# Five moves of order in a fused attention and feed-forward kernel: spread stores, another order of splits, another choice of banks

## The chip, the cores and the metric

One core of a Trainium2 chip runs the kernel. The metric is the device time of one execution in microseconds (us); less is better. TensorE (PE in the profile) does the matmuls, VectorE (DVE), ScalarE (ACT) and GpSimd (POOL) the elementwise work, and SyncE (SP) issues every DMA of this kernel, in the order of the program.

## The reference, cut to what matters

The input x has 2048 rows of 576 features. The output is a mix of two branches: `g*a + (1-g)*b`, with g a sigmoid of a dot product of each row with a gate vector.

- Branch a is attention with a compressive memory: 32 heads of 18 features and 4 segments of 512 rows. Each segment has causal softmax attention within itself, and reads a memory M (and its normaliser z) summed over the segments before it. The two are mixed per head and multiplied by `wo`.
- Branch b is a gated feed-forward layer: `(silu(x @ w_gate) * (x @ w_up)) @ w_down`, with 4608 hidden features.

All inputs and the output are float32. The kernel keeps that precision on TensorE by splitting each operand into a rounded high part and a remainder, a "split": ACT copies the high part, DVE subtracts it from the source to get the low part. Three products (high by high, high by low, low by high) then stand for one.

## The kernel before, in words

**First stage (lines 283 to 685).** The projections for queries, keys and values, and the memory. Near its end the operands for the first half of the feed-forward layer are made: `w_make` splits the weights, `first_sum` (POOL) and `first_split` (ACT and DVE, through `split`, lines 131 to 133) make the seven x operands.

**Main stage (lines 688 to 1126).** The feed-forward layer runs over `seq`: two halves of the rows (1024 each), and in each half 36 units f of 128 hidden features, so 72 units. One unit is seven products (`seven`, line 1010, a Strassen-like scheme: seven products of sums and differences instead of eight). One `seven` is six matmuls at line 1015 and one at line 1018, all with 512 columns. After each `seven` (and twice after the sixth) the unit calls `tick`, so eight ticks, k = 0 to 7. A tick issues some DMAs and then calls `beat`.

**The beat (line 959)** is where the order of the work is written by hand. It first runs the functions that are due (`defer(k, fn)` puts fn into the list of the k-th beat from now; items of one list run in the order in which they were deferred). Then, if groups of the down projection are waiting, it runs some of them (`SHARE[k]`: none in beats 0 and 1, two in beats 2 and 3, three in beats 4 to 7); between them it advances the attention generator `att_gen` by one step. A unit with groups takes 12 attention steps; a unit without groups about 2 to 3, since only five of its beats count and each earns 0.57 (first half) or 0.47 (second half) of a step.

**Groups.** Every third unit f (`q == 0`) `feed` puts 16 groups on the list: the down projection of the three units before. A group (`down_parts`, line 848) is nine matmuls of line 862 into one bank, then DVE adds the bank to `ya` (line 872) and the bank is free.

**Attention.** 64 units u of 5 logits tiles each. `att_gen` takes six steps for a unit, n = 0 to 5. A step does `p_bank` (line 753: DVE cast, POOL subtraction), `e_bank` (ACT exponentials, line 742), `s_bank` (line 717: the matmuls of the logits, line 724, and the DVE reduction of line 730; in steps 0 to 4), `v_unit` (line 763: the 40 small matmuls of lines 772 and 773 with the values, then a DVE reduction, line 779; in step 5, for the unit before) and `x_bank` (line 759: a DMA transpose into a `pt` tile, of which there are seven).

**Banks.** The PSUM has eight banks. Banks 0 to 2 serve the seven products. `group_tile` takes the least recently taken of banks 3, 4 and 7. `ts_tile`, for logits and values, takes the least recently taken of 5, 6, 7, 3, 4 when no groups wait; of 5, 6, 7 while all 16 groups still wait (beats 0 and 1); of 5 and 6 afterwards. A tile of `ts_tile` counts as taken four ticks of the clock later than it was, a group's one.

**Between the halves.** After unit 35 of the first half come ten beats of their own (lines 1109 to 1117, `BREAK`), in which the last 16 groups of the half run. The first of these beats also runs three groups at once in two cuts: the products of the first two units, then those of unit 35, whose split is due in that same beat. Meanwhile `x_second` (line 979) makes the x operands of the second half. Its four tables give the beat of each step, with offset 0 on the first tick of unit 35, 8 on the first of the ten beats and 18 on the first tick of the second half: `LOADS` (raw pieces of x from memory; z = 0 and 1 are two sets), `SUMS` (POOL, line 991), `PARTS` (the splits: ACT line 132, DVE line 133). The ten beats' groups also leave eight finished tiles of `ya` on the list `stores` (line 874); `tick` issues them all when k is 0. The weights of units 0 and 1 of the second half come ready-made from memory (`w_fetch`, line 704, into `wo_` tiles, source `wc`); the last of unit 0, for its seventh product, is issued in the first tick of the second half, behind the stores.

**Last stage.** The output projection, 16 tiles of rows (lines 1128 to 1161).

Of the kernel before, what the change touches and what calls it, by code (L numbers as in the profile page):

```python
# [26 lines left out]
NSEG = 4  # L27
# [8 lines left out]
CH = 3  # L36
# [12 lines left out]
SHARE = (0, 0, 2, 2, 3, 3, 3, 3)  # L49
BREAK = 10  # L50
LOADS = ((-3, 0, 0), (-2, 0, 1), (3, 1, 0), (4, 1, 3), (4, 0, 3), (5, 0, 2), (5, 1, 1), (6, 1, 2))
SUMS = ((2, 0, 1), (9, 0, 4), (10, 1, 1), (11, 1, 4), (13, 1, 2), (14, 1, 6), (17, 0, 2), (18, 0, 6))
PARTS = ((1, 0, 0), (4, 0, 1), (10, 1, 0), (12, 1, 5), (12, 1, 3), (13, 1, 1), (14, 1, 2), (15, 1, 4), (16, 1, 6),
         (16, 0, 5), (17, 0, 3), (18, 0, 2), (19, 0, 4), (20, 0, 6))
FIRST = (9, 10, 11, 15, 16, 17, 18)
SLOT = (0, 3, 2, 1, 4, 6, 5)
RPOS = (0, 1, 4, 2, 5, 6, 3)
# [9 lines left out]
def gated_mix(ctx, tc, xT, xrest, wf, wfr, wfh, wd, wv, wo, beta, cmask, ident, bmask, out):  # L67
# [44 lines left out]
    y_tile = banks(2)  # L112
    taken = {}
    clock = [0]

    def soonest(ids, held):
        n = min(ids, key=lambda i: taken.get(i, 0))
# [2 lines left out]
        return n  # L120

    def ts_tile(shape=(P, L)):
        ids = (5, 6, 7, 3, 4) if not groups else (5, 6, 7) if groups[0][0] < FT // CH - 1 and len(groups) == 16 else (5, 6)
        return ps.tile(list(shape), F32, name=f"bank{soonest(ids, HELD)}")

    def group_tile(shape=(P, L)):
# [157 lines left out]
    with ExitStack() as st:  # L284
# [249 lines left out]
        def first_split(j, z):  # L534
            XO[j][z] = x_slot(SLOT[j], z)
            split(XO[j][z][:, 0], XO[j][z][:, 1], rx[{1: (0, z), 4: (1, z), 2: (1, 2 + z), 6: (0, 2 + z)}[j]])
# [144 lines left out]
        flush()  # L681
        while start[0][0] < 8:
            start.pop(0)[1]()
        for z in range(2):
            first_split(6, z)


    with ExitStack() as st:
# [3 lines left out]
        def defer(k, fn):  # L692
            while len(due) < k:
                due.append([])
            due[k - 1].append(fn)
# [100 lines left out]
        def att_gen():  # L796
            N = 12 * NB

            def at(t):
                return 5 * (t // 6) + t % 6 if 0 <= t < N and t % 6 < 5 else None  # L800

            for tau in range(N + 10):
                u, n = divmod(tau, 6)
                if n == 2 and sends:
                    nc.sync.dma_start(*sends.pop(0))
                if 1 <= n <= 3 and u + 1 < 2 * NB:
                    for d in stack_loads(u + 1)[3 * n - 3:3 * n]:
                        nc.sync.dma_start(*d)
                if n == 2 and u > 1 and u % 2 == 1 and (u - 3) // 2 < NB:
                    o_step((u - 3) // 2)  # L810
                z = at(tau - PL)
                if z is not None:
                    p_bank(z)
                z = at(tau - 1)
                if z is not None:
                    e_bank(z)
                z = at(tau)
                if z is not None:
                    s_bank(z)
                if n == 5 and 1 <= u <= 2 * NB:  # L820
                    v_unit(u - 1)
                    if u % 4 == 1 and u // 4 + 1 < 4 * NSEG:
                        v_fetch(u // 4 + 1)
                z = at(tau - XL)
                if z is not None:
                    x_bank(z)
                yield
            for z in sends:
                nc.sync.dma_start(*z)
# [191 lines left out]
        draw = {}  # L1021
        for o, fn in start:
            defer(o - 7, fn)
        for pos, (half, f) in enumerate(seq):
            if f == 0:
                yas[half] = yp.tile([P, 8, D], F32, name="ya")
# [1 line left out]
            nxt = seq[pos + 1] if pos + 1 < len(seq) else None  # L1028
            if q == 0 and f:
                groups += feed(half, f - 1)  # L1030
            plan = []
            if not nxt:
                plan.append((3, lambda: early.append(c_tr(*tiles.pop(0)))))
# [17 lines left out]
            def tick():  # L1051
                k = step[0]
                step[0] += 1
                if k == 0:
                    while stores:
                        nc.sync.dma_start(*stores.pop(0))
                if half == 0:
                    if (q, k) in ((0, 3), (1, 3), (2, 2)):
                        draw[f] = d_load(f)
# [156 lines left out]
```

## Time and profile before

| what | value |
|---|---|
| time, median of 3 runs | 1736.47 us (1733.69 to 1738.83) |
| the profiled execution's own time | 1734.02 us |
| its span, first to last instruction | 1732.2 us |
| granted TensorE clock, mean | 0.999 |
| busy: PE, DVE, ACT, POOL | 1713.1, 1373.7, 1092.4, 936.7 us |
| mean share of the DMA engines on the core's queue | 76.6% |

A row of the timeline gives the start (us from the span's start), the duration, engine, line, operation, what is written and read, how many instructions were merged, and in brackets the idle time before it with what ended it. TensorE's matmuls are pipelined: a matmul of 512 columns is shown with about 0.39 us, though the next one starts about 0.23 us after it. So a wait of TensorE is read from start to start; the bracket shows only what is left after the shown end. In the list of waits each row gives the engine and line that waited, what it waited for, the total in us, how often, and the longest.

In the first half unit 0 starts at 220.87 us; the ten beats between the halves run from about 925.4 to 947.7 us, and the second half's unit 0 starts at 947.69 us.

### The profile page before, as it was taken

Reading aid. Unit: us, or ns where it says so; the run is one execution under the profiler, and the core shown is the slowest. Engines: PE = TensorE matmul, PEld = TensorE weight load, DVE = VectorE, ACT = ScalarE, POOL = GpSimd, SP = SyncE. Lnnn points to the kernel's source line nnn. Section 1 sums busy time; section 2 is a strip of 40 time slices with the busy share of each in tenths; the row PEclk is TensorE's granted clock in tenths of the full one; section 3 lists DMA queues with packets and bytes.
Section 4 is the critical chain, followed back from the end, with each engine's and each line's share of the span. In section 5 each row is a group of like instructions: output and inputs, shape, how many; then the busy total and the mean of one; then the engine's idle time right before and its main releaser. Section 6 shows DMA issues by size and latency. Waiting matters only on the chain.

```text
span 1732.2 us, 34907 instructions
## 1 busy us (share of the span) xinstructions
PE 1713.1 (99%) x11868; PEld 1479.3 (85%) x11868; DVE 1373.7 (79%) x3231; ACT 1092.4 (63%) x2195; POOL 936.7 (54%) x1194
## 2 busy tenths in 40 slices
PE   9999999999999999999999999999999999999999
PEld 7899978888888888887888788888888888888899
DVE  6667588888898889898989677788788777888655
ACT  7766585776677577667756756665765576566511
POOL 4424645666666556565666455555555555555221
PEclk9999999999999999999999999999999999999999
DMA  8654499999898898897979976876778677766544
GB/s 285 227 194 154 146 311 191 223 218 193 208 227 194 178 213 198 190 194 200 206 150 260 273 161 146 183 180 157 157 181 181 137 161 182 163 144 166 160 146 137
DMA packets 524002, 328.05 MB, mean 189 GB/s; under 512 B 411184, under 2 KB 460336, under 8 KB 523824
## 3 DMA queue, kind: packets, MB, share of 16 engines
q1 hardware_dynamic: 523824, 325.83, 76.6%
q8 instruction: 93, 1.52, 0.4%
q14 instruction: 85, 0.70, 0.1%
HBM read 165.76 MB, written 76.09 MB: 140 GB/s over the span
## 4 chain that ended last, share of the span: by engine, by line
PE 80%; ACT 6%; DVE 6%; DMA 3%; issue 2%; POOL 1%; SPq 1%; DVEq 0%; ACTq 0%; POOLq 0%
PE bank L1015 31%; PE bank L862 25%; PE bank L155 10%; PE bank L1018 5%; PE bank L724 4%; PE bank L772 2%; PE bank L773 1%; ACT L1092 1%; PE bank L410 1%; DVE scr L730 1%; DVE hl L957 1%; DVE p L756 1%; PE bank L456 1%; ACT L1008 1%; DVE xo L133 1%
## 5 line engine op out<-in xcount | busy, mean ns | idle before, releaser
L757 POOL TENSOR_TENSOR p<-pe,p 128x512 f16<-128x512 f32 x320 | 374.0, 1169 | 451.0 <-DVE p L756 431.3
L862 PE MATMUL bank<-dw,hh 128*128 128x320 f32 (+1 forms) x2304 | 489.7, 305 | 2.6 <-DVE ya L872 2.1
L862 PEld LDWEIGHTS bank<-dw,hh 128*128 128x128 f32 x2304 | 380.5, 190 | 16.7 <-DVE ya L872 5.7
L742 ACT ACTIVATE pe<-bank,mb 128x512 f32<-128x512 f32 (+3 forms) x512 | 246.0, 522 | 218.7 <-DVE mb L730 213.3
L862 PE MATMUL bank<-dw,hl 128*128 128x320 f32 (+1 forms) x1152 | 340.3, 295 | 0.2 <-DVE hl L133 0.2
L730 DVE CUSTOM_DVE_ANT_0 scr<-bank,cm 128x512 bf16<-128x512 f32 (+3 forms) x512 | 246.5, 481 | 7.8 <-PE bank L724 1.1
L862 PEld LDWEIGHTS bank<-dw,hl 128*128 128x128 f32 x1152 | 217.9, 189 | 0.4 <-DVE hl L133 0.4
L872 DVE TENSOR_TENSOR ya<-bank,ya 128x320 f32<-128x320 f32 x352 | 157.6, 453 | 71.5 <-PE bank L862 70.6
L1018 PE MATMUL bank<-xr,rh 128*128 128x512 f32 x504 | 196.5, 390 | 0.0
L750 POOL TENSOR_SCALAR_AFFINE_SELECT pe<-pe 128x256 f32<-128x256 f32 (+1 forms) x320 | 151.1, 473 | 30.4 <-ACT pe L742 20.1
L756 DVE CAST p<-pe 128x512 f16<-128x512 f32 x320 | 149.2, 466 | 0.0
L260 POOL TENSOR_TENSOR ws<-raw 128x256 f32<-128x256 f32 x140 | 123.5, 882 | 17.3 <-DMA raw<-in_wf_dram 5.1
L724 PE MATMUL bank<-kst,qst 108*128 108x512 bf16 (+3 forms) x512 | 125.5, 306 | 0.0
L1018 PEld LDWEIGHTS bank<-xr,rh 128*128 128x128 f32 x504 | 94.7, 188 | 20.5
L957 DVE TENSOR_TENSOR hl<-row,hh 128x512 fp32r<-128x512 f32 x120 | 101.9, 849 | 10.8 <-ACT hh L956 10.5
L1085 ACT ACTIVATE row<-bank 128x512 f32<-128x512 f32 x72 | 43.1, 598 | 83.9 <-PE bank L1018 83.8
L1092 ACT ACT_TABLE_LOAD x72 | 92.4, 1283 | 1.3
L1090 DVE TENSOR_TENSOR row<-bank,row 128x512 f32<-128x512 f32 x72 | 49.6, 689 | 54.6 <-ACT bank L1089 54.4
L1008 ACT ACT_TABLE_LOAD x70 | 89.8, 1283 | 1.0
L1089 ACT ACTIVATE bank<-bank 128x512 f32<-128x512 f32 x72 | 42.0, 584 | 67.2 <-PE bank L1018 66.8
L155 PE MATMUL bank<-xo,qhi 128*128 128x512 f32 x264 | 83.1, 396 | 0.3 <-ACT vps L395 0.3
L1075 ACT ACTIVATE bank<-bank 128x512 f32<-128x512 f32 x72 | 41.6, 578 | 66.2 <-PE bank L1018 66.2
(2167 smaller groups left out, 4137.6 us busy)
## 6 DMA issues: line engine op xcount, KB each, us to landing
raw<-in_wf_dram SPq DMA_DIRECT2D x140, 256.0 KB
rh<-rc SPq DMA_DIRECT2D x72, 336.0 KB
dc<-dw SPq DMA_DIRECT2D x36, 576.0 KB
dw<-dc SPq DMA_DIRECT2D x36, 576.0 KB
stk<-q SPq DMA_DIRECT2D x32, 384.0 KB
draw<-in_wd_dram SPq DMA_DIRECT2D x36, 288.0 KB
rc<-rt SPq DMA_DIRECT2D x42, 224.0 KB
vd<-vps SPq DMA_DIRECT2D x8, 912.0 KB
```

The costliest lines, as they stand in the source:

```text
L155: nc.tensor.matmul(t, st[n], mv[n], start=(n == 0), stop=(n == 13))
L260: (nc.gpsimd.tensor_sub if sub else nc.gpsimd.tensor_add)(src[j], p(), q())
L724: nc.tensor.matmul(t[:, c:c + w], qs[:KR, pr, P * i:P * i + P], ks[:KR, pr, 0:w], start=True, stop=True)
L730: nc.vector.tensor_tensor_reduce(scr[:, :w], t[:, c:c + w], cm[:, L - w:L], -SCALE, 3.0e38, OP.add, OP.min, m[:, k:k + 1])
L742: nc.scalar.activation(pe[:, c:c + w], t[:, c:c + w], AF.Exp, bias=m[:, k:k + 1], scale=SCALE)
L750: nc.gpsimd.affine_select(d, d, pattern=pat, compare_op=OP.is_ge, fill=0.0, base=0, channel_multiplier=1)
L756: nc.vector.tensor_copy(p[:, 0], pe)
L757: nc.gpsimd.tensor_sub(p[:, 1], pe, p[:, 0])
L862: nc.tensor.matmul(ts[m], p, q[:, cs], start=(n == 0), stop=(n == 3 * CH - 1))
L872: nc.vector.tensor_add(ya[:, i, cs], t, ya[:, i, cs])
L1015: nc.tensor.matmul(t, w[:, p, z], x[z][:, q], start=first and n == 0, stop=False, skip_group_check=True)
L1018: nc.tensor.matmul(t, rem[:, RPOS[j]], XR[j], start=False, stop=True, skip_group_check=True)
```

## The change: what it does

1. **Stores.** `tick` issues one waiting store in each odd tick, instead of all of them in tick 0. The eight stores go out in ticks 1, 3, 5 and 7 of units 0 and 1 of the second half.
2. **The order of x.** `SUMS` and `PARTS` get other offsets and another order. Ten splits lie in the ten beats instead of nine, and two follow in ticks 0 and 1 of the second half instead of three in ticks 0 to 2. The first two splits of the set z = 0 move to offsets 8 and 9. All sums lie before offset 17, two of them earlier than before. `LOADS` stays.
3. **Bank 7 first.** The first tile that `ts_tile` gives out after `feed` is bank 7 (unless bank 7 is the one taken last, or the groups are the half's last); after that, while groups wait, only banks 5 and 6.
4. **Values ahead of the next step's logits.** Where no groups wait at step 5, `v_unit` (with the `v_fetch` that hangs on it) is held and runs in step 0 of the next unit, after that step's exponentials and ahead of its logits. Where groups wait, it stays in step 5.
5. **The last split of x.** `first_split(6, z)`, two splits, ran at the end of the first stage; it is now due in the second beat of unit 0, so after that unit's second product.

```diff
-SUMS = ((2, 0, 1), (9, 0, 4), (10, 1, 1), (11, 1, 4), (13, 1, 2), (14, 1, 6), (17, 0, 2), (18, 0, 6))
-PARTS = ((1, 0, 0), (4, 0, 1), (10, 1, 0), (12, 1, 5), (12, 1, 3), (13, 1, 1), (14, 1, 2), (15, 1, 4), (16, 1, 6),
-         (16, 0, 5), (17, 0, 3), (18, 0, 2), (19, 0, 4), (20, 0, 6))
+SUMS = ((2, 0, 1), (9, 0, 4), (11, 0, 2), (12, 1, 1), (13, 1, 4), (14, 0, 6), (14, 1, 2), (16, 1, 6))
+PARTS = ((1, 0, 0), (4, 0, 1), (8, 0, 5), (9, 0, 3), (10, 1, 0), (11, 1, 5), (12, 1, 3), (13, 0, 4), (14, 0, 2),
+         (15, 1, 1), (16, 1, 4), (17, 1, 2), (18, 0, 6), (19, 1, 6))
...
+    fed = []
...
     def ts_tile(shape=(P, L)):
-        ids = (5, 6, 7, 3, 4) if not groups else (5, 6, 7) if groups[0][0] < FT // CH - 1 and len(groups) == 16 else (5, 6)
+        ids = (5, 6) if groups else (5, 6, 7, 3, 4)
+        if fed and groups[0][0] < FT // CH - 1 and max(taken, key=taken.get) != 7:
+            ids = (7,)
+        fed.clear()
         return ps.tile(list(shape), F32, name=f"bank{soonest(ids, HELD)}")
...
-        for z in range(2):
-            first_split(6, z)
...
+            held = []
             for tau in range(N + 10):
...
+                if n == 5 and 1 <= u <= 2 * NB:
+                    held.append(u)
+                if held and (groups or n == 0):
+                    v = held.pop()
+                    v_unit(v - 1)
+                    if v % 4 == 1 and v // 4 + 1 < 4 * NSEG:
+                        v_fetch(v // 4 + 1)
                 z = at(tau)
                 if z is not None:
                     s_bank(z)
-                if n == 5 and 1 <= u <= 2 * NB:
-                    v_unit(u - 1)
-                    if u % 4 == 1 and u // 4 + 1 < 4 * NSEG:
-                        v_fetch(u // 4 + 1)
...
+        for z in range(2):
+            defer(2, lambda z=z: first_split(6, z))
...
                 groups += feed(half, f - 1)
+                fed.append(f)
...
-                if k == 0:
-                    while stores:
-                        nc.sync.dma_start(*stores.pop(0))
+                if k % 2 and stores:
+                    nc.sync.dma_start(*stores.pop(0))
```

## The prediction

> **What bounds the kernel now.** I read the page's busy times and chain first, then the list of TensorE's waits, then the timeline around each long one.
>
> ```profile
> PE 1713.1 (99%) x11868; PEld 1479.3 (85%) x11868; DVE 1373.7 (79%) x3231; ACT 1092.4 (63%) x2195; POOL 936.7 (54%) x1194
> ...
> PE 80%; ACT 6%; DVE 6%; DMA 3%; issue 2%; POOL 1%; SPq 1%; DVEq 0%; ACTq 0%; POOLq 0%
> ```
>
> ```profile
> PE bank L1015 <- DMA wo__13415<-wc: 3.0, 1, 3.0
> PE bank L862 <- DVE ya L872: 2.1, 3, 0.9
> PE bank L1015 <- ACT bank L1075: 1.7, 5, 0.6
> PE bank L1015 <- DVE bank L1082: 1.6, 2, 1.1
> ...
> PE bank L1015 <- DVE xo L133: 0.9, 1, 0.9
> PE bank L772 <- DMA pt<-p: 0.9, 1, 0.9
> ```
>
> TensorE is busy 99% of the span and holds 80% of the chain that ended last. The change takes no matmul away, so all it can win is TensorE's waits, and these rows hold most of them: about ten microseconds in single, short pieces. The sum below is made from start to start in the timeline, since the list shows less than a wait costs.
>
> **The last split of x (part 5).** In unit 0 the third product adds to the bank that line 1075 copies, and waits for that copy.
>
> ```profile
> 223.93 0.39 PE L1018 MATMUL bank<-xr,rh 128*128 128x512 f32 x1
> 224.87 1.66 PE L1015 MATMUL bank<-xo,wo__2473 128*128 128x512 f32 x6 [0.56 <-ACT bank L1075]
> ```
>
> ```profile
> 223.20 1.14 ACT L132 ACTIVATE xo<-ph 128x512 fp32r<-128x512 f32 x2
> 224.25 0.57 ACT L1075 ACTIVATE bank<-bank 128x512 f32<-128x512 f32 x1
> ```
>
> ```profile
> 224.24 1.41 DVE L133 TENSOR_TENSOR xo<-ph,xo 128x512 fp32r<-128x512 f32 x2
> ...
> 226.87 0.70 DVE L1082 TENSOR_TENSOR bank<-bank,row 128x512 f32<-128x512 f32 x1 [0.88 <-PE bank L1018]
> ```
>
> The two high copies (1.14 us) stand right ahead of it on ACT. Moved two beats on, they leave line 1075 free to run from 223.20 to 223.8, before the second product ends at 224.15. The gap from 223.93 to 224.87 is 0.94 us where two matmuls without a wait start 0.22 apart (394.72 and 394.94 below): **0.7 us** gained. Behind them, DVE's two subtractions (1.41 us) now stand between the second product and line 1082. That instruction was idle for 0.88 us before, and its user is the fifth product, one product later; the cover is thin, so the bounds are 0 and 0.8.
>
> **Bank 7 first (part 3).** Of the groups in beat 3, the first is the half's third.
>
> ```profile
> 267.66 0.39 PE L1018 MATMUL bank<-xr,rh 128*128 128x512 f32 x1
> 268.13 0.56 PE L862 MATMUL bank<-dw,hh 128*128 128x320 f32 x2
> ```
>
> ```profile
> 389.57 0.39 PE L1018 MATMUL bank<-xr,rh 128*128 128x512 f32 x1
> 390.60 0.56 PE L862 MATMUL bank<-dw,hh 128*128 128x320 f32 x2 [0.65 <-DVE ya L872]
> ...
> 394.72 0.39 PE L1018 MATMUL bank<-xr,rh 128*128 128x512 f32 x1
> 394.94 0.45 PE L862 MATMUL bank<-dw,hh 128*128 128x320 f32 x2
> ```
>
> ```profile
> 1594.09 0.39 PE L1018 MATMUL bank<-xr,rh 128*128 128x512 f32 x1
> 1594.58 0.56 PE L862 MATMUL bank<-dw,hh 128*128 128x320 f32 x2
> ```
>
> I worked the choice of banks through the code, call by call. Where a tile of the attention took bank 7 in beat 1, it still counts as taken in beat 3, and the third group gets the bank of the first again, whose addition to `ya` is late on a full DVE. That is so in 4 passages of the first half and all 11 of the second; where bank 7 was taken in beat 0, the third group gets bank 7 and does not wait. Three of the 15 are the row of 2.1 us: at 389.57 the gap is 1.03 instead of 0.22, so 0.81 lost where the list shows 0.65; with 0.16 more for each, 2.6 us for the three. Five more are short, the first and the last shown here: 0.47 and 0.49, so 0.26 lost each, 1.3 together. In each of the eight the first pair of matmuls is also 0.1 longer (0.56 for 0.45): 0.8. Together 4.7. The change makes the third group get bank 7 in all of them. I take **4.2**, since what follows on the same DVE may be late next; the bounds are 2.4 and 4.7.
>
> **Between the halves (parts 1 and 2).** Here lies the longest wait.
>
> ```profile
> 951.17 0.48 PE L1015 MATMUL bank<-xo,wo__13172 128*128 128x512 f32 x1
> 952.57 0.73 PE L1015 MATMUL bank<-xo,wo__13172 128*128 128x512 f32 x2 [0.92 <-DVE xo L133]
> ```
>
> ```profile
> 959.77 0.39 PE L1018 MATMUL bank<-xr,rh 128*128 128x512 f32 x1
> 963.11 2.60 PE L1015 MATMUL bank<-xo,wo__13415 128*128 128x512 f32 x6 [2.95 <-DMA wo__13415<-wc]
> ```
>
> ```profile
> 952.24 5.49 SPq L1056 DMA_DIRECT2D ffd<-ya  x8
> 957.82 0.88 SPq L709 DMA_DIRECT2D wo__13415<-wc  x1
> ```
>
> ```profile
> 959.80:963.00 3.20, 0.36 (x2) 0.00 (x0) 0.17 (x1) 3.16 (x5) 0.00 (x0) 1.00 1.00 235
> 963.10:966.90 3.80, 3.79 (x10) 2.97 (x11) 0.66 (x2) 0.09 (x1) 0.00 (x0) 0.55 1.12 288
> ```
>
> SP spends 5.49 us on issuing the eight stores and only then issues the last weights of unit 0. With the stores in odd ticks it issues them at 952.3; if they take as long as now (957.82 to 963.11, 5.3 us) they are there at 957.6, before the seventh product could start; behind no stores it should be sooner. The stores' own issue, about 0.69 us each, stays on SP, now between the loads of two units; `ya` is not written again before unit 3, so nobody waits for them. The wait is 3.34 less 0.22: 3.1 us. After it the granted clock is 0.55 for 3.8 us, which costs 45% of that, 1.7 us; it goes with the wait. The third product's wait for the low part of x is 1.40 less 0.22, 1.2 us, and the new order has its parts done earlier. That makes 6.0.
>
> Two things speak against getting it all.
>
> ```profile
> 924.53 0.43 SPq L986 DMA_DIRECT2D raw<-in_xT_dram  x1
> ```
>
> ```profile
> 926.27 3.76 DMA wo__13005<-in_xT_dram
> ```
>
> ```profile
> 926.34 0.58 ACT L1094 ACTIVATE row<-bank 128x512 f32<-128x512 f32 x1
> 927.20 0.63 ACT L132 ACTIVATE hh<-row 128x512 fp32r<-128x512 f32 x1 [0.28 <-DVE row L1100]
> ```
>
> ```profile
> 927.96 0.49 PE L862 MATMUL bank<-dw,hh 128*128 128x320 f32 x2
> 928.61 0.42 PE L862 MATMUL bank<-dw,hl 128*128 128x320 f32 x1 [0.16 <-DVE hl L133]
> ```
>
> First, the split at offset 8. It was deferred in unit 34, so in the list of the first beat between the halves it stands ahead of unit 35's own split, on which the groups' second cut waits already. Its source is the raw piece issued at 924.53; a neighbour of the same size needed 3.76 us (the chain's row), so it lands near 928.3. ACT would come to it at 926.92 and stand until 928.3 with unit 35's split behind it, which then begins 1.65 us later than 927.20; DVE's extra subtraction comes on top. TensorE's wait at 927.96 grows by about 1.7, of which the next wait gives a little back: I take 1.5 lost, bounds 0 and 2.2.
>
> ```profile
> 925.00:947.00 22.00, 21.62 (x188) 20.46 (x187) 21.32 (x45) 12.58 (x23) 16.46 (x15) 1.00 1.10 315
> ```
>
> ```profile
> L133 DVE TENSOR_TENSOR xo<-raw,xo x7: 683/824/1675, 917.2 to 956.1; 128x512 fp32r<-128x512 f32 x7
> ```
>
> ```profile
> 955.49 0.69 DVE L1082 TENSOR_TENSOR bank<-bank,row 128x512 f32<-128x512 f32 x1
> ```
>
> Second, DVE. It is busy 21.3 of the 22 us between the halves, and gets one subtraction more there (0.68 to 1.68 us each) and none less before line 1082 of the new unit. That instruction ended at 956.2, hidden by a unit of values, which part 4 moves out of this unit. Without the third product's 1.2 us, the fifth product could start at 954.5 and has to wait for line 1082. I take 1.0 lost, bounds 0 and 2.4. The sum here is 6.0 less 2.5: **3.5** gained; bounds 6.0 gained and, if the new waits slow the clock once more (1.7), 0.3 lost.
>
> [...]
>
> **Values one step later (part 4).** By the schedule 25 of the 64 value units move, by one step; the same matmuls run elsewhere. Six go into beat 0 of a unit with groups, six from the end of such a unit into the next, the others one or two beats on in their unit. I find no wait of TensorE that they cover or uncover for certain: the copy of line 1075 (1.7 us in the list) is late ahead of both the old places and the new ones. I take 0, with 1 gained and 2 lost as bounds. What it adds is a wait on SP: `x_bank` of the same step needs the `pt` tile that these values read, so the transpose is held until TensorE has done them, and the loads of logits operands, raw weights and stores stand behind it.
>
> **The sum.** 0.7 + 4.2 + 3.5 + 0 = 8.4 us. The profiled execution took 1734.02 us, so it would take 1725.6. It lies 2.45 below the median of the runs shown, 1736.47; from that median the forecast is **1728.1 us**.
>
> **The rivals.**
>
> *Nothing is given back.* The raw piece lands early enough and DVE keeps up: 0.7 + 4.7 + 6.0 = 11.4, so 1725.1. For it: SP is relieved and the sums come three or four beats ahead of their splits. Against it: the full DVE.
>
> *DVE becomes the bound between the halves.* All of that stretch's gain goes, 0.3 more is lost: 0.7 + 4.2 - 0.3 = 4.6, so 1731.9. For it: 21.3 of 22 us and the spread of its durations.
>
> *The stores do not do what they are spread for.* Their bytes stay among the loads of unit 1's weights, and the wait of 3.1 + 1.7 comes back at one of its products: 8.4 less 4.8, so 1732.9. Against it: those loads are issued several beats ahead.
>
> *Slower: the transposes wait for the values.*
>
> ```profile
> SPq L761 <- PE bank L773: 3.7, 4, 1.4
> ```
>
> This wait exists four times, at 0.9 us. If each of the 25 moved values puts one on SP and the queue has no lead, what stands behind it is late by as much, and TensorE with it, as once already for `pt` (0.9): 25 times 0.9 is 22.5, less 8.4 is 14.1 lost, so 1750.6. It decides from about 10 of the 25. Against it: a transpose is used five steps after its issue.
>
> **How the numbers follow.** Two measurements of this kernel can tell about 0.3% (5.2 us) from no change: below 1731.3 is faster, above 1741.7 slower. The forecast has 0.48, nothing given back 0.18, the full DVE 0.14, the stores 0.10, slower 0.10. Faster: nearly all of the first, all of the second, a third of the two others, 0.72. Slower 0.10, the rest 0.18. The forecast alone has 1724 to 1732. The range goes from 1722 (all bounds of gain and the runs' own scatter) to 1737, where the smallest gains of each part leave almost nothing.
>
> **What would show it.** Right: no wait for `wc` weights at the second half's seventh product, no clock below 1 behind it, the row L862 <- L872 gone, none for line 1075 in unit 0. New: ACT standing before the first x split between the halves, a wait for line 1082 in the second half's first unit. Wrong: TensorE waiting for `pt` or for weights in many units, or SP's row for line 773 grown from 4 to some 25 with TensorE's waits beside it.

## The result, and the profile after

| kernel | median | lowest to highest | runs | ratio to before, 95% interval |
|---|---|---|---|---|
| before | 1735.64 us | 1733.58 to 1738.83 | 6 | |
| changed | 1729.8 us | 1728.27 to 1730.42 | 6 | 0.9964 [0.9953, 0.9974] |

The changed kernel is faster by 0.36%. The forecast was 1728.1 us and its range held the time, but most terms of the sum came out at another size. In the profiled execution (1729.77 us against 1734.02) the span fell from 1732.2 to 1728.1, by 4.1 us, where the sum said 8.4.

In the changed kernel lines have moved: 1015 is now 1021, 1018 is 1024, 862 is 868, 872 is 878, 724 is 726, 742 is 744, 772 and 773 are 774 and 775, 132 and 133 are 136 and 137, and the evictions 1075, 1082 and 1089 are 1083, 1090 and 1097. The kernels of the experiments have their own numbering, a few lines off from one of these two. Units are counted through here, 0 to 71: unit 36 is the second half's unit 0. The page's busy times, after:

```profile
PE 1710.3 (99%) x11868; PEld 1481.7 (86%) x11868; DVE 1365.0 (79%) x3231; ACT 1092.5 (63%) x2195; POOL 940.0 (54%) x1194
```

The list of TensorE's waits, after (what waited, for what, us in all, times, longest):

```profile
PE bank L868 <- ACT hh L136: 2.1, 1, 2.1
PE bank L726 <- ACT pe L744: 1.7, 3, 1.0
...
PE bank L774 <- ACT pe L744: 1.2, 2, 0.8
...
PE bank L1021 <- DMA wo__13533<-wc: 0.4, 1, 0.4
```

Before's two longest rows, 3.0 us for a piece of `wo` and 2.1 for `ya`, are gone, and so is the third product's wait for `xo` (0.9). In their place stand waits that were not there: 2.1 for ACT's split `hh`, 1.7 and 1.2 for the exponentials of line 744. The waits for the three evictions stay much the same, 3.9 us together after 4.3. The change took away the waits it aimed at; a good part of them came back elsewhere.

**Where the time went.** I compared when each unit's last matmul (line 1018, now 1024) starts in the two traces. Up to the end of unit 34 the changed kernel is 0.56 us ahead, at the end of unit 35 0.95, after unit 39 only 1.33 and at the end 4.16. So the stretch between the halves, where the longest waits were, gave about 0.4 us, and most of the gain lies in the second half, where nothing large was seen to wait. Three places show it.

*Between the halves.* TensorE, then ACT, in the changed kernel's timeline:

```profile
926.86 0.31 PE L868 MATMUL bank<-dw,hl 128*128 128x320 f32 x1
929.27 0.56 PE L868 MATMUL bank<-dw,hh 128*128 128x320 f32 x2 [2.10 <-ACT hh L136]
```

```profile
928.07 0.63 ACT L136 ACTIVATE xo<-raw 128x512 fp32r<-128x512 f32 x1 [2.10 <-DMA raw<-in_xT_dram]
928.60 0.61 ACT L136 ACTIVATE hh<-row 128x512 fp32r<-128x512 f32 x1
```

ACT comes to the x split of offset 8, stands 2.10 us for the raw piece, and unit 35's own split `hh` starts at 928.60 behind it (927.20 before). TensorE's gap is 2.41 us from start to start, 2.26 more than the 0.15 of a neighbour. Then the clock falls (start and end, busy of PE, PEld, DVE, ACT, POOL, then PEclk, DMA share, GB/s):

```profile
929.20:932.00 2.80, 2.35 (x24) 1.93 (x25) 2.77 (x10) 2.77 (x6) 1.56 (x3) 0.86 0.94 273
932.00:936.00 4.00, 4.00 (x47) 4.00 (x45) 4.00 (x6) 3.21 (x7) 3.03 (x3) 0.67 1.13 285
```

In slices of 1 us from 930 to 936 the granted clock reads 1.00, 0.62, 0.50, 0.50, 0.68 and 1.00. As an estimate, a window costs its length times what its clock lacks to 1: 0.39 for 2.8 us at 0.86 and 1.32 for 4 us at 0.67, so 1.7 us of TensorE's work is lost. Before, 0.55 over 3.8 us was the same 1.7 us behind the wait for `wo`: that clock loss did not go, it moved with the longest wait.

*Unit 0.* The third product follows the second without a wait, as forecast, but two later products wait longer. The first of them, the fifth, follows the logits:

```profile
223.90 0.39 PE L1024 MATMUL bank<-xr,rh 128*128 128x512 f32 x1
224.12 1.52 PE L1021 MATMUL bank<-xo,wo__2473 128*128 128x512 f32 x6
...
227.30 0.39 PE L726 MATMUL bank<-kst,qst 108*128 108x512 bf16 x1
227.74 1.66 PE L1021 MATMUL bank<-xo,wo__2628 128*128 128x512 f32 x6
...
230.82 0.39 PE L1024 MATMUL bank<-xr,rh 128*128 128x512 f32 x1
231.74 0.96 PE L1021 MATMUL bank<-xo,wo__2681 128*128 128x512 f32 x3 [0.53 <-ACT bank L1097]
```

DVE ahead of the fifth product:

```profile
226.99 0.69 DVE L1090 TENSOR_TENSOR bank<-bank,row 128x512 f32<-128x512 f32 x1
```

Line 1090 stands behind the two subtractions of the last split and ends at 227.68; the fifth product starts 0.44 us after the logits' matmul, where it started 0.04 after it before. ACT ahead of the seventh product, after and then before:

```profile
230.78 0.42 ACT L268 ACTIVATE wo__2722<-ws 128x256 fp32r<-128x256 f32 x1 [2.38 <-DMA wc<-wo__2473]
```

```profile
230.92 0.42 ACT L264 ACTIVATE wo__2722<-ws 128x256 fp32r<-128x256 f32 x1 [1.64 <-DMA wc<-wo__2473]
```

ACT's copy of the weights waits for a transfer that ends at nearly the same time in both; TensorE comes earlier, so the wait is 0.74 longer (2.38 for 1.64), and the eviction right behind it on ACT (line 1097) holds TensorE 0.70 us beyond the usual 0.22. By the starts of line 1024, the lead of 0.89 us behind the third product (0.72 of it that wait) is 0.57 behind the fifth and 0.14 at the end of unit 0: DVE takes 0.32 of it and ACT 0.43.

*The first half's groups.* In unit 21 the third group no longer waits: line 868 follows line 1024 after 0.23 us. Some beats later line 726 waits.

```profile
630.54 0.39 PE L1024 MATMUL bank<-xr,rh 128*128 128x512 f32 x1
630.77 0.45 PE L868 MATMUL bank<-dw,hh 128*128 128x320 f32 x2
...
645.81 0.28 PE L868 MATMUL bank<-dw,hl 128*128 128x256 f32 x1
647.06 0.38 PE L726 MATMUL bank<-kst,qst 108*128 108x512 bf16 x1 [0.98 <-ACT pe L744]
```

ACT at the second place:

```profile
644.79 1.28 ACT L1014 ACT_TABLE_LOAD   x1
...
646.19 0.82 ACT L744 ACTIVATE pe<-bank,mb 128x256 f32<-128x256 f32 x2
```

The new logits need bank 5 or 6, whose last exponentials stand on ACT behind a table load of 1.28 us.

### The profile page after: what moved, and what is told of

Read it like the earlier page. It is cut to its first block, busy times and chain, and to the rows that moved or that the text cites. A ratio compares the mean times of both kernels' runs of the same rounds, so it can differ in the third digit from the quotient of the medians.

```text
span 1728.1 us, 34897 instructions
## 1 busy us (share of the span) xinstructions
PE 1710.3 (99%) x11868; PEld 1481.7 (86%) x11868; DVE 1365.0 (79%) x3231; ACT 1092.5 (63%) x2195; POOL 940.0 (54%) x1194
## 3 DMA queue, kind: packets, MB, share of 16 engines
q8 instruction: 93, 1.52, 0.4%
## 4 chain that ended last, share of the span: by engine, by line
PE 77%; ACT 7%; DMA 5%; DVE 5%; issue 3%; POOL 2%; SPq 1%; DVEq 0%; ACTq 0%; POOLq 0%
PE bank L1021 30%; PE bank L868 23%; PE bank L159 10%; PE bank L1024 5%; PE bank L726 3%; PE bank L774 2%; PE bank L775 1%; ACT L1100 1%; ACT pe L744 1%; PE bank L414 1%; ACT L1014 1%; DMA rc<-rt 1%; POOL ws L264 1%; DMA raw<-in_wf_dram 1%; POOL p L759 1%
## 5 line engine op out<-in xcount | busy, mean ns | idle before, releaser
L963 DVE TENSOR_TENSOR hl<-row,hh 128x512 fp32r<-128x512 f32 x120 | 107.3, 894 | 10.1 <-ACT hh L962 9.5
L264 POOL TENSOR_TENSOR ws<-raw,ws 128x256 f32<-128x256 f32 x70 | 58.3, 833 | 45.8 <-DVE wo__22572 L271 10.3
L374 POOL TENSOR_TENSOR q<-qr,q 128x512 bf16<-128x512 f32 x36 | 44.5, 1235 | 70.4 <-ACT q L373 63.9
```

The costliest lines, as they stand in the source:

```text
L264: (nc.gpsimd.tensor_sub if sub else nc.gpsimd.tensor_add)(src[j], p(), q())
```

## The experiments

Twelve kernels, each timed in five rounds beside the kernel before. Ratios are to the kernel before, with 95% intervals; a difference between two experiments is less certain than either, about 2 us (the medians of the kernel before, timed beside them, run from 1734.6 to 1736.0). A trace is a single execution, and its time can lie some us off its kernel's median.

### Stores

**All stores in the first beat again.**

```diff
-                if k % 2 and stores:
-                    nc.sync.dma_start(*stores.pop(0))
+                if k == 0:
+                    while stores:
+                        nc.sync.dma_start(*stores.pop(0))
```

> Base: the changed kernel (1729.8) with all stores of a unit issued in its first beat again, as before. Theory A (the spread took the 3.1 us wait for a piece of wo away, and the lowered clock behind it): that wait comes back at the unit where the old kernel had it, 1732 to 1734. Theory B (the bytes only moved: the waits of 0.5 and 0.54 us for pieces of wo in unit 37 and those of 0.8 us in unit 39 are the same bytes later, and the new order had already moved the splits away from them): 1729.3 to 1730.5, with the waits in units 37 and 39 gone or changed by as much as another one grows.

1734.93 us, ratio 0.9998 [0.9989, 1.0007]. The whole gain is gone; theory A holds, by more than it said. TensorE's timeline and two windows of that kernel:

```profile
962.25 0.39 PE L1024 MATMUL bank<-xr,rh 128*128 128x512 f32 x1
967.26 1.19 PE L1021 MATMUL bank<-xo,wo__13418 128*128 128x512 f32 x2 [4.63 <-DMA wo__13418<-wc]
```

```profile
962.20:967.00 4.80, 0.44 (x2) 0.01 (x1) 0.25 (x1) 3.43 (x5) 0.00 (x0) 0.90 1.28 302
967.00:972.70 5.70, 5.44 (x13) 4.30 (x14) 1.62 (x3) 0.00 (x0) 0.30 (x1) 0.50 0.98 305
```

The wait for the last weights of the second half's unit 0 is back, at 4.79 us beyond the usual 0.22, and the clock is at 0.50 over the 5.7 us behind it. It is longer than the 3.1 of before because SP issued these weights 0.23 us before TensorE was ready for them (962.24, before 2.2 us ahead), and they took 5.0 us; this execution took 1737.66 us, 2.7 above its kernel's median.

**The spread alone, on the kernel before.**
```diff
-                if k == 0:
-                    while stores:
-                        nc.sync.dma_start(*stores.pop(0))
+                if k % 2 and stores:
+                    nc.sync.dma_start(*stores.pop(0))
```

> Base: the kernel before (1735.6) with the spread of the stores alone. Theory A (the 3.1 us wait for a piece of wo between the halves goes, and the lowered clock behind it, 1.7 us; the third product's wait of 1.2 us stays): 1730.5 to 1731.5, the granted clock at 1.00 where it had fallen. Theory B (the next piece on the same queue is late in its place, as the waits in units 37 and 39 of the changed kernel hint): 1732.5 to 1734.

1731.15 us, ratio 0.9974 [0.9965, 0.9984]: within theory A. The clock is at 1.00 from 959.8 to 966.9. Unit 37 has one new wait for a piece of `wo`, 0.93 us:

```profile
962.51 0.39 PE L1018 MATMUL bank<-xr,rh 128*128 128x512 f32 x1
963.67 0.70 PE L1015 MATMUL bank<-xo,wo__13450 128*128 128x512 f32 x2 [0.77 <-DMA wo__13450<-wc]
```

So the bytes do press on the next unit, as theory B said, but for a fifth of the price, and behind its wait of 0.93 us the clock stayed at 1.00 (963.1 to 966.9). In the two traces unit 36 is 4.2 us shorter than before and units 37 to 39 are 1.7 longer, so a part of what is won is met again there. The spread is worth 4.5 us by the medians, about the 4.8 of the prediction.

### The order of x

**The old tables, everything else changed.**

```diff
-SUMS = ((2, 0, 1), (9, 0, 4), (11, 0, 2), (12, 1, 1), ...
-PARTS = ((1, 0, 0), (4, 0, 1), (8, 0, 5), (9, 0, 3), (10, 1, 0), ...
+SUMS = ((2, 0, 1), (9, 0, 4), (10, 1, 1), (11, 1, 4), ...
+PARTS = ((1, 0, 0), (4, 0, 1), (10, 1, 0), (12, 1, 5), (12, 1, 3), ...
```

> Base: the changed kernel (1729.8) with the old tables for the order of x between the halves (SUMS and PARTS of before); stores spread, bank 7, values and the last split as changed. Theory A (the new order costs about what it brings: it took away a 1.2 us wait of the third product and the half clock, and brought a 2.2 us wait of unit 35's products for ACT's split hh with some 1.5 us of lowered clock behind it): without the new order those 2.2 us and the lowered clock go, the third product's 1.2 us come back, and the stores, still spread, keep the 3.1 us wait for a piece of wo away; 1728 to 1729.3, no PE wait of over 1 us at the start of unit 35 on ACT's hh. Theory B (the new order is what gave the gain between the halves): 1731 to 1732.

1726.92 us, ratio 0.9956 [0.9943, 0.9968]: theory A, 1.1 us below its lower end. ACT's timeline, the window of the whole stretch and TensorE at the third product:

```profile
927.58 0.63 ACT L136 ACTIVATE hh<-row 128x512 fp32r<-128x512 f32 x1 [0.27 <-DVE row L1108]
```

```profile
925.00:947.00 22.00, 21.61 (x186) 20.40 (x185) 21.38 (x44) 12.68 (x21) 16.84 (x15) 1.00 1.09 297
```

```profile
952.95 1.40 PE L1021 MATMUL bank<-xo,wo__13172 128*128 128x512 f32 x5 [0.92 <-DVE xo L137]
```

The split `hh` runs as soon as its source is there, the clock stays at 1.00 (0.92 in the changed kernel over the same 22 us), and the third product waits 1.2 us again: its first matmul starts at 951.54, and the next one not until 952.95. Giving back 1.2 us to be rid of 2.3 and 1.7 is the better bargain.

**The new order on the spread alone.** The kernel before with the spread and the new tables.

> Base: the kernel before (1735.6) with parts 1 and 2, the spread stores and the new order of x, and nothing else; stores alone gave 1731.2. Theory A (the new order costs more than it brings whatever the other parts do: a 2.2 us wait of unit 35's products for ACT's split hh and a lowered clock behind it, against a third product's wait of 1.2 us saved): 1732.5 to 1733.5. Theory B (the order's price comes from the other parts, values or bank 7, which make TensorE early there): 1729.5 to 1731, with the wait for hh under 0.5 us.

1733.98 us, ratio 0.9991 [0.9982, 1.0], against 1731.15 for the spread alone. Theory A, a little beyond its range. From TensorE's list of waits:

```profile
PE bank L862 <- ACT hh L132: 2.1, 1, 2.1
```

The same wait, and behind it the same clock (0.86 over 2.8 us and 0.67 over 4.0, as in the changed kernel), come without values and banks. By the medians the order costs 2.9 us in the company of the other parts and 2.8 with the spread alone; by the ratios it is 1.4 and 3.0. In the traces the stretch from the end of unit 35 to that of unit 39 is 3.1 and 2.6 us longer with it.

**The two early splits one beat later.**

```diff
-(8, 0, 5), (9, 0, 3), (10, 1, 0)
+(9, 0, 5), (10, 0, 3), (10, 1, 0)
```

> The changed kernel with the two splits at offsets 8 and 9 put at 9 and 10, so that unit 35's own split no longer stands behind one that waits for its raw piece. Theory A (that order makes the wait of 2.26 us at 926.86 us and the low clock after it, about 1.5 us): the wait falls to the 0.3 to 0.4 us that it was before the change, the clock stays at 1, 3 us or so are gained: 1726 to 1727.5. Theory B (ACT and DVE are simply full there): the wait moves to a later beat and the time stays at 1729 to 1730.

1729.73 us, ratio 0.9965 [0.9952, 0.9979], the changed kernel's time and inside theory B's range. The wait for `hh` is gone (0.33 us for the low part `hl` is left, as there was before), and another takes its place at 933.85, 2.46 us beyond the usual 0.21, again with a lower clock behind it, 0.63 over 4.5 us. From the list of waits and from the windows:

```profile
PE bank L868 <- DVE ya L878: 2.3, 1, 2.3
```

```profile
936.50:941.00 4.50, 4.48 (x22) 4.48 (x23) 3.85 (x9) 1.21 (x2) 2.79 (x2) 0.63 1.15 298
```

So it is not the one late raw piece: with the splits in these two places too, one of the engines is late for something. Here it is DVE, which does two x subtractions and that of line 963 back to back, from 932.32 to 936.1, ahead of the addition to `ya` that TensorE waits for.

### Bank 7

**The old choice of banks, everything else changed.**
```diff
-        ids = (5, 6) if groups else (5, 6, 7, 3, 4)
-        if fed and groups[0][0] < FT // CH - 1 and max(taken, key=taken.get) != 7:
-            ids = (7,)
-        fed.clear()
+        ids = (5, 6, 7, 3, 4) if not groups else (5, 6, 7) if groups[0][0] < FT // CH - 1 and len(groups) == 16 else (5, 6)
```

> The changed kernel with part 3 undone: the old choice of banks. Theory A (the third group's wait was worth 4.7 us, but in the first half 3.4 us of it came back as waits for banks 5 and 6 in beats 3 to 6): 1730.8 to 1731.8, the waits of the products' groups on the addition to ya are back, those of logits and values on ACT's exponentials fall from 2.9 us to under 1. Theory B (bank 7 is worth all of it, and the waits on the exponentials come from the held values): 1734 to 1735, with the waits on the exponentials still there.

1729.55 us, ratio 0.9961 [0.9949, 0.9974]. Both theories missed: nothing is lost. Theory A's waits are as it said, those for `ya` back and those for the exponentials gone, but they balance. The third group's wait of unit 21 is back (lines 1021 and 865 are the changed kernel's 1024 and 868),

```profile
630.58 0.39 PE L1021 MATMUL bank<-xr,rh 128*128 128x512 f32 x1
632.29 0.56 PE L865 MATMUL bank<-dw,hh 128*128 128x320 f32 x2 [1.33 <-DVE ya L875]
```

1.49 us beyond 0.22, and the two waits of the same unit for exponentials, 0.53 and 1.14 us in the changed kernel, are gone; unit 21 takes the same time to 0.04 us.

**Bank 7 in the second half alone, on the old order of x.**

```diff
-        if fed and groups[0][0] < FT // CH - 1 and max(taken, key=taken.get) != 7:
-            ids = (7,)
-        fed.clear()
+        if groups and 0 in fed:
+            ids = (5, 6, 7) if groups[0][0] < FT // CH - 1 and len(groups) == 16 else (5, 6)
+        elif 1 in fed:
+            if groups and groups[0][0] < FT // CH - 1 and max(taken, key=taken.get) != 7:
+                ids = (7,)
+            fed.clear()
...
-                fed.append(f)
+                fed[:] = [half]
```

> Base: the changed kernel with the old tables for the order of x between the halves (1726.9), and bank 7 given to the first logits tile after a feed in the second half alone; in the first half the banks are chosen as before. Theory A (in the first half the bank only moves the wait: TensorE, let go earlier by the third group, meets ACT's exponentials, 0.2 to 1.1 us at a time; in the second half it keeps about 1.2 us): the first half ends 0.9 us earlier than with bank 7 in both halves, the second keeps its gain; 1725.8 to 1726.3, no wait of TensorE for an exponential over 0.3 us, the waits for the third group's tile back in the first half alone. Theory B (the bank has no net worth in either half): 1726.6 to 1727.6.

1726.71 us, ratio 0.9946 [0.9934, 0.9959], against 1726.92 with bank 7 in both halves: inside theory B's range and not theory A's, 0.2 us of a possible 0.9. One wait for an exponential of 0.51 us stayed (unit 24), which A excluded. In the trace the units of the second half take as long as with bank 7 in both halves, to 0.05 us, but for the second and the last one. The first half is 2.1 us shorter there, 0.8 of it in unit 4, where TensorE waits for a transpose, 0.3 to 1.9 us long in the traces of this case. So the traces lean to theory A, and by the times a gain of 0.9 us in the first half cannot be told from none.

### Values

**Values in their old place.**
```diff
-                if n == 5 and 1 <= u <= 2 * NB:
-                    held.append(u)
-                if held and (groups or n == 0):
-                    v = held.pop()
-                    ...
                 z = at(tau)
                 if z is not None:
                     s_bank(z)
+                if n == 5 and 1 <= u <= 2 * NB:
+                    v_unit(u - 1)
+                    ...
```

> The changed kernel (median 1729.8 us) with part 4 undone: values run in step 5 again. Theory A (values ahead of logits save TensorE one turn from attention matmuls back to the products): in the two traces the units into or through which values moved, and which had no wait, are 0.08 to 0.17 us shorter each, and 25 value units moved, so undoing it costs 2 to 4 us: 1732 to 1734, and the waits on banks 5 and 6 stay as they are. Theory B (part 4 is worth nothing, as forecast; the gain of the second half comes from bank 7): 1729.3 to 1730.3. SP's waits on the value matmuls (28.6 us in 18) fall back to about 4 us in either.

1731.0 us, ratio 0.9973 [0.9964, 0.9982], between the expectations: by the medians part 4 is worth about 1.2 us. The execution of the trace took 1733.14 us, 2.1 above the median; in it TensorE waits 1.89 us for a transpose in unit 4, with the clock at 0.57 over the 4 us behind it (last section), so that trace can't price part 4 in the first half.

**Values held, but behind the next step's logits.**

```diff
-                if held and (groups or n == 0):
-                    v = held.pop()
-                    ...
                 z = at(tau)
                 if z is not None:
                     s_bank(z)
+                if held and (groups or n == 0):
+                    v = held.pop()
+                    ...
```

> The changed kernel with values held as in part 4, but run behind the logits of step 0 instead of ahead of them. If the saved turn is what counts (theory A), it does not matter which of the two comes first: 1729.3 to 1730.5. If it counts that the values cover the wait for the logits' bank (theory C), the gain of part 4 goes: 1732 to 1734.

1732.27 us, ratio 0.9982 [0.9973, 0.9991]. The matmuls and the beats are those of the changed kernel; only the order of values and logits within a beat differs, and the gain is gone. That is theory C's range; theory A, as it was put, fails, for it does matter which comes first. But C's reason is not seen: TensorE waits 2.0 us for the exponentials ahead of line 726 with the logits first and 1.7 in the changed kernel. (The execution of this trace took 1737.67 us, 5.4 above the median, so only like units are compared.) In unit 47 before, a product has the values ahead of it and a later one the logits. A product with nothing ahead of it goes from one line 1018 to the next in 1.59 us, and its six matmuls take 1.52 (the row at 224.12 above).

```profile
1160.91 0.39 PE L1018 MATMUL bank<-xr,rh 128*128 128x512 f32 x1
...
1162.19 1.65 PE L1015 MATMUL bank<-xo,wo__16265 128*128 128x512 f32 x6
1163.68 0.39 PE L1018 MATMUL bank<-xr,rh 128*128 128x512 f32 x1
...
1165.29 0.39 PE L1018 MATMUL bank<-xr,rh 128*128 128x512 f32 x1
...
1167.13 0.39 PE L1018 MATMUL bank<-xr,rh 128*128 128x512 f32 x1
```

After, values and logits stand ahead of one product:

```profile
1162.42 0.39 PE L1024 MATMUL bank<-xr,rh 128*128 128x512 f32 x1
...
1163.71 0.38 PE L726 MATMUL bank<-kst,qst 108*128 108x512 bf16 x1
...
1165.30 0.39 PE L1024 MATMUL bank<-xr,rh 128*128 128x512 f32 x1
```

With the logits first:

```profile
1167.89 0.39 PE L1024 MATMUL bank<-xr,rh 128*128 128x512 f32 x1
1168.12 0.39 PE L726 MATMUL bank<-kst,qst 108*128 108x512 bf16 x1
...
1170.87 0.39 PE L1024 MATMUL bank<-xr,rh 128*128 128x512 f32 x1
```

From line 1024 to the next, values and logits take 2.88 us in the changed kernel and 2.98 with the logits first. Before, values took 2.77 and logits 1.84 in two products, 4.61, which is 2.88 + 1.59 (a bare product) + 0.14. Behind the values the six fp32 matmuls take 1.65 for 1.52: the step from these small bf16 matmuls to an fp32 product costs about 0.1. Values right ahead of the logits don't pay it, and the logits alone add about 0.25 to a product (1.84 less 1.59), little more than a matmul's 0.23. With the logits first, the values stand right ahead of the product again and pay. In units of the changed kernel that hold moved values and no wait, the gain on before is 0.08 to 0.17 us, some 20 times; with the logits first, twenty such units are 0.06 to 0.13 us longer than in the changed kernel, 2.1 us together.

**Values ahead of the logits in every unit.**

```diff
-                if held and (groups or n == 0):
+                if held and n == 0:
```

> Base: the changed kernel (1729.8) with the values held to the next step ahead of the logits in every unit, in those that feed groups of transposes too (the changed kernel does so only in units without groups). Theory A (values ahead of logits save TensorE 0.09 to 0.17 us a unit, because no fp32 product then follows the values' small matmuls): some 39 more units of the 72 gain as much, 3.5 to 6.6 us: 1723 to 1726.5. Theory B (in units with groups the transposes stand between the values and the product already, so there is no such turn to save, or the later values make the division's tile, the bank or the stores of a unit late): 1729.3 to 1732.

1728.14 us, ratio 0.9962 [0.9948, 0.9976]: 1.7 us less than the changed kernel by the medians, 1.2 below B's range and 1.6 above A's. In the second half nine of the eleven units with groups gain 0.05 to 0.26 us each. In the first half the third group waits for the addition to `ya` again at three units (21, 24 and 27), 0.9 to 1.1 us each, which A left out.

### The last split

**Back to the end of the first stage.**

```diff
+        for z in range(2):
+            first_split(6, z)
...
-        for z in range(2):
-            defer(2, lambda z=z: first_split(6, z))
```

> Base: the changed kernel (1729.8) with x's last split back at the end of the first stage. Theory A (the chain meets a transfer of wo that lands at a fixed time, so most of the 0.76 us between the second and the third product is idle that is had later anyway): 1729.6 to 1730.2; the wait of 0.76 us between the second and third product comes back, and PE's wait for ACT's copy on the other eviction line near 231 us falls from 0.70 to about 0.26. Theory B (the 0.76 us are worth what they last): 1730.4 to 1730.7.

1729.45 us, ratio 0.997 [0.9959, 0.9982], 0.35 us below the changed kernel's median and 0.15 below theory A's range. Theory A by the trace: the third product waits 0.67 us again, and the eviction that held TensorE for 0.70 us waits less, since ACT stands 1.58 us for the same transfer and not 2.38. It ends at nearly the same time as in the two kernels above:

```profile
230.66 0.42 ACT L268 ACTIVATE wo__2722<-ws 128x256 fp32r<-128x256 f32 x1 [1.58 <-DMA wc<-wo__2473]
```

### Together

**Stores spread, old order of x, bank 7 in the second half, values ahead in every unit.**

> Base: the previous kernel of this call, with the values held ahead of the next logits in units with groups too. If what that brought on top of the changed kernel (1.3 us on the medians; by the units some 0.1 us in most units with groups of the second half, in the first half gains and waits that cancel) adds to the rest: 1724.5 to 1725.3. Rival: with the third group on its old bank in the first half, the late values make the group's wait for the copy of ya longer there (0.9 to 1.1 us at three units already): 1726 to 1727.

1725.23 us, ratio 0.9941 [0.9927, 0.9954], as the first expectation said. It is the fastest of all; its interval touches that of the changed kernel, 0.9964 [0.9953, 0.9974], so its lead over it, 4.6 us by the medians, is likely and not certain to its size. The rival's longer waits are there, 0.82 and 0.88 us new at units 24 and 27, and the rest outweighs them.

## Why the prediction came out as it did

**Part 5, 0.7 expected, 0.14 measured.** The wait went as forecast. DVE's thin cover did not quite hold: line 1090 took 0.32 us, inside the bounds of 0 and 0.8 that the prediction gave. The step left out is what is late after that: ACT, waiting for a transfer that ended only 0.14 us earlier (the copy behind it starts at 230.78, 230.92 before), which took 0.43. The kernel with the old place confirms that the part is worth nothing that can be measured.

**Part 3, 4.2 expected, about nothing measured.** This is the step that failed most. The eight passages were the right ones and their waits went. "What follows on the same DVE may be late next" looked at the wrong engine: in the first half the next limit is ACT's exponentials in banks 5 and 6, and TensorE meets it 15 us later with nearly the same wait (0.53 and 1.14 us in unit 21, for 1.49 with the old banks). In the second half no such wait shows, and the trace keeps about 1.2 us there (0.41, 0.37, 0.3 and less at units 60, 69, 63 and others). Part of the eight waits goes away without part 3 too, most likely with the values' new places: without it five third-group waits are left (units 3, 21, 30, 60, 69), and those of units 9, 39 and 63 are gone. So parts 3 and 4 overlap. By the medians, adding both and part 5 to stores and order gained 4.2 us (1733.98 to 1729.8), all but the values 3.0 (to 1731.0) and all but the banks 4.4 (to 1729.55). How large each is alone stays open within 2 us.

**Parts 1 and 2, 3.5 expected, about 0.4 measured between the halves.** The removed waits were sized rightly: 3.1 for `wo`, 1.7 of clock, 1.2 for the third product, and the stores alone brought 4.5. The loss on ACT was forecast with its mechanism, but its price was too low, 1.5 for 2.3 us. That the time agrees (the raw piece was to land near 928.3, and ACT went on at 928.07) is luck. TensorE was 0.95 us ahead by then, and SP began to issue the piece at 923.22 instead of 924.53:

```profile
923.22 1.13 SPq L992 DMA_DIRECT2D raw<-in_xT_dram  x1
```

ACT had it 4.85 us after that, where the forecast took 3.76 from a neighbour. Seen from TensorE the piece came 0.7 us later than forecast, and that is what the price was short of. Behind the new wait the clock fell as behind the old one (0.86 over 2.8 us and 0.67 over 4.0; 0.55 over 3.8 before), 1.7 us more, which stood only in a bound. That is the step that failed: "if the new waits slow the clock once more" was the likely case. The loss at line 1082 was 0.4 (expected 1.0), and unit 37's weights cost 0.50 and 0.54, the stores' rival at a fifth of its price. Adding up: 6.0 less 2.3, 1.7, 0.4 and 1.0 is 0.6.

**Part 4, 0 expected, 1 to 3 gained.** The medians give about 1.2 (1731.0 without it). In the trace the units with moved values and no wait give some 2.6 us together and unit 35, whose wait for line 1090 shrank from 1.26 to 0.87, another 0.4; the first half's new waits take part of it. The prediction counted the same matmuls elsewhere and left out that their neighbours matter. The slower rival did not come: SP waits for the values much oftener, and no wait of TensorE for a transfer is over 0.54 us.

```profile
SPq L763 <- PE bank L775: 28.6, 18, 4.5
```

This row was 3.7 us and 4 times before, and it is 3.3 and 3 with the values in their old place. TensorE's wait for `pt` is there once, as before. With values held everywhere the row grows to 57.2 us and 35 times, in a kernel no slower.

**The full DVE as a bound.** Its rival took 3.8 us off the forecast's gain between the halves. The stretch gave up nearly as much, but by ACT's wait and the clock: DVE was busy 19.27 of the 22 us, less than before.

```profile
925.00:947.00 22.00, 19.53 (x164) 18.70 (x164) 19.27 (x39) 11.13 (x20) 14.44 (x13) 0.92 1.09 282
```

The spread of durations that spoke for that rival was no wider with two of POOL's sums earlier: one and the same x subtraction took 683/824/1675 ns (shortest, median, longest) before and 680/719/1543 after. All fourteen x subtractions of the stretch took 13.9 us before and 13.0 after, though single ones grew (one from 1.00 to 1.47).

```profile
L137 DVE TENSOR_TENSOR xo<-raw,xo x7: 680/719/1543, 916.2 to 953.2; 128x512 fp32r<-128x512 f32 x7
```

**The sum.** In the trace 0.1 (part 5), some 0.5 (banks: about 1.25 won in the second half, 0.8 lost in the first), 0.4 (between the halves) and 3 (values) make the 4.1 us of the span, where 0.7, 4.2, 3.5 and 0 made 8.4. That the forecast still came within 1.7 us is luck in good part: three terms were too high and the fourth too low, and the forecast was set from the median shown then, 1736.47, while its sum was read from an execution of 1734.02, 1.6 below the median of six. The execution of after lies at its median. With six runs each the medians stand 5.8 us apart, so 1.7 us of that gain is in no term that the traces show.

## What to carry to other kernels

When a wait goes on an engine that is 99% busy, follow that engine to the next instruction that depends on something it does not drive, a transfer (ACT's copy behind one started at 230.66, 230.78 and 230.92 in three kernels here, after ACT had stood 1.58, 2.38 and 1.64 us) or another engine's queue, and count only the difference; the wait of 0.72 us kept 0.14 here, that of 1.49 us nothing. Price a TensorE wait by its length and by what the clock does behind it: those of 1.89, 2.26, 2.46 and 3.1 us cost about 1.7 us more here, those of 0.93, 1.49 and 1.59 did not, so breaking up one long wait pays even if the bytes are still late. When work is moved to an earlier beat, look first at what stands behind it in the same engine's list: unit 35's `hh` began 1.40 us later here (928.60 for 927.20), behind a split that stood 2.10 us.

## What the runs showed of the hardware

**The clock's loss came in one size.** Reckoned as above, it was about 1.7 us each behind TensorE's waits of 2.26 (changed kernel: 0.86 over 2.8 us and 0.67 over 4.0), 2.46 (the two splits a beat later: 0.63 over 4.5) and 3.1 us (before: 0.55 over 3.8); in and behind the 4.79 us wait it was 0.48 + 2.85 and a little more (0.90 over 4.8, 0.50 over 5.7), twice that. The row of 5.7 us at 0.50 is the lowest rate in any of these windows. The clock fell too, by the same 1.7 us, behind a wait of 1.89 us for a transpose in unit 4 of the kernel with the values in their old place, the shortest wait in these traces behind which a fall was seen:

```profile
291.51 0.20 PE L774 MATMUL bank<-v,pt 128*128 128x57 bf16 x1 [1.75 <-DMA pt<-p]
```

```profile
291.50:295.50 4.00, 3.99 (x24) 3.99 (x25) 1.12 (x2) 0.00 (x0) 0.81 (x2) 0.57 1.24 180
```

Behind waits of 1.49 us (old banks, 632.3 to 636.0) and 1.59 (the spread alone, unit 21) it stayed at 1.00; the second:

```profile
632.91 0.41 PE L862 MATMUL bank<-dw,hh 128*128 128x320 f32 x1 [1.42 <-DVE ya L872]
```

```profile
633.00:637.00 4.00, 4.00 (x26) 3.66 (x27) 3.92 (x12) 1.16 (x2) 3.27 (x8) 1.00 1.11 219
```

Where between 1.59 and 1.89 us the fall begins, and whether anything but the length of the wait decides, was not tried.

**Small matmuls right ahead of a product cost TensorE time.** About 0.1 us for each step from the values' small bf16 matmuls to an fp32 product shows in the rows of unit 47 above; nothing in the list of waits shows it. That the logits, bf16 too but of 512 columns, cost only 0.02 there beyond a matmul's own 0.23 speaks against the type alone. Whether the few columns (57 and 38) or the loads of their weights make it was not tried.
